# PV of the last three heads between the quarters: one decode block on one Trainium2 core

## The chip, the core and the metric

The kernel runs on one core of one Trainium2 chip. A core has a matrix engine (TensorE, PE in the profile, with its weight loads as PEld), VectorE (DVE), ScalarE (ACT), GpSimd (POOL) and SyncE (SP, which here issues nearly all DMA transfers). The engines run side by side, each works through its own queue in order, and they wait for each other through semaphores. PE reads SBUF and writes PSUM; DVE and ACT read both. The metric is device microseconds of the core. The time before is 532.45 us, the median of three runs between 530.86 and 533.08.

## The reference

One token for each of four sequences: a layer norm, then attention over the last 2048 positions of a cache of 8192 and, in parallel, a SwiGLU block, both added to the input.

```python
# B, Sq, D = 4, 1, 640;  Hq = Hkv = 32, Sk = 8192, Dh = 192;  F = 1536;  all bfloat16
W = min(4096, max(256, Sk // 4))                       # 2048
q = (x @ wq).reshape(B, Sq, Hq, Dh).transpose(0, 2, 1, 3)
k = k_cache[:, :, Sk - W:, :];  v = v_cache[:, :, Sk - W:, :]
p = _softmax(einsum("bhqd,bhkd->bhqk", q, k) * Dh ** -0.5)
o = einsum("bhqk,bhkd->bhqd", p, v)
A = o.transpose(0, 2, 1, 3).reshape(B, Sq, Hq * Dh) @ wo
Bo = (_silu(xn @ w1) * (xn @ w3)) @ w2                 # xn: layer norm of x
return x + A + Bo
```

Every head has its own keys and values: 32 heads x 4 sequences x 2048 positions x 192 numbers of two bytes, for K and for V, 201 MB of the 223 MB that the kernel reads.

## The kernel before, in words

**Layout.** A head's keys lie in one SBUF tile of 128 partitions: partition q holds 64 positions (NJ) of sequence q mod 4, 192 numbers each. Values lie alike. There are two key tiles (KBUFS) and three value tiles (VBUFS). SP issues one DMA for the keys and one for the values of a head (`load_k`, `load_v`; the values of the last and the third last head come in two halves).

**Scores.** A head is worked in four quarters of 16 positions (GQ, JQ); quarter u is head u // 4. `mult` (L231) multiplies keys by the query on DVE, `adder` (L242) adds the six 32-wide slices with six identity matmuls on PE, and `reduce_quarter` (L250) sums the last 32 on DVE. After a head's four quarters comes the softmax chain: `chain_lmax` (L254, DVE), `chain_tr` (L259, PE transpose), `chain_gmax` (L264 and L267, DVE: the maximum per sequence, and gneg, its negative scaled), `chain_bc` (L272 on PE, then L275 and the exponential L278 on ACT), and `chain_z` (L286, DVE), which spreads the weights over a one-hot of the sequence.

**PV.** `pv` (L295) multiplies the weights with the values: 24 matmuls a head, in three 32-row strips of one PSUM bank. The bank holds for each of eight positions j and four sequences all products, of which only those with the same j on both sides are wanted. `pv_diag` masks the bank (L303, o_m) and sums over j (L306, o_sb) on DVE, `ge_sum` (L322) adds the strips' sequences on PE. `ge_tot` (L311) adds the softmax denominators, `ge_rec` (L317) inverts them. Four heads form a group: `ge_turn` (L326, L328) scales and transposes (og, oT), and `ge_proj` (L212) multiplies by the group's rows of wo into the accumulator acc. `ffn_out` adds the SwiGLU block's products with w2 (L212 too) in three pieces.

**Order.** The order of work is written out by hand: `add(slot, phase, fn, ...)` puts a step into a slot, and slots are emitted one after the other, by phase within a slot. Engines keep the order of emission. There is one slot for each quarter (NU = 128) and some behind. A head's PV comes 8 slots (L) after its first quarter, mask and sum one slot later, the strip sums another slot later. The last three heads have their own places:

```python
ends = {H - 3: (NU - 3, NU - 2, NU - 1), H - 2: (NU + 2, NU + 3, NU + 4), H - 1: (NU + 6, NU + 7, NU + 7)}
```

Each triple gives the slots of PV, mask and sum, and strip sums. The last loads are issued in slot NU - 6: values of heads 30 and 31, then w2's first eight of twelve chunks, wo of the last two groups, w2's next three chunks and its last. They follow each other in one queue. At the end acc is cast to bfloat16 on DVE (L447), and two DMAs, from SP and ACT, write the two halves of the output's columns.

## Time and profile before

| | |
|---|---|
| median of three runs | 532.45 us |
| the profiled execution's own time | 533.66 us |
| its span, first to last instruction | 531.9 us |
| mean granted clock of PE | 0.89 |
| PE busy | 370.4 us, 70% |
| DVE busy | 392.5 us, 74% |
| ACT busy | 29.0 us, 5% |
| DMA, main queue, share of 16 engines | 97.7% |
| HBM read | 222.96 MB, 419 GB/s over the span |

The profile shows one execution. Busy time of an engine is an average over a start, a long even middle part of 32 heads and an end; shares say little about the end. A row such as "o_sb<-o_m 96x64 f32<-96x512 f32" names the tile written and the tile read with partitions and elements. The granted clock is the share of full speed at which PE was allowed to run. Where the text gives single times, they are us from the start of the span.

### The profile page before, as it was taken

Reading aid. Unit: us, or ns where it says so; the run is one execution under the profiler, and the core shown is the slowest. Engines: PE = TensorE matmul, PEld = TensorE weight load, DVE = VectorE, ACT = ScalarE, POOL = GpSimd, SP = SyncE. Lnnn points to the kernel's source line nnn. Section 1 sums busy time; section 2 is a strip of 40 time slices with the busy share of each in tenths; the row PEclk is TensorE's granted clock in tenths of the full one; section 3 lists DMA queues with packets and bytes.
Section 4 is the critical chain, followed back from the end, with each engine's and each line's share of the span. In section 5 each row is a group of like instructions: output and inputs, shape, how many; then the busy total and the mean of one; then the engine's idle time right before and its main releaser. Section 6 shows DMA issues by size and latency. Waiting matters only on the chain.

```text
span 531.9 us, 4826 instructions
## 1 busy us (share of the span) xinstructions
PE 370.4 (70%) x1986; PEld 143.5 (27%) x1987; DVE 392.5 (74%) x498; ACT 29.0 (5%) x110; POOL 1.1 (0%) x8
## 2 busy tenths in 40 slices
PE   2766567677658776468778676567868776876865
PEld 1322222232213322223222222223222322222323
DVE  3178776788948876887858878788768888878853
ACT  2121000000000000000000000000000000000000
POOL 0000000000000000000000000000000000000000
PEclk9989997979978889998977979899787899799777
DMA  8999999999999999999999999999999999999991
GB/s 359 440 425 432 439 427 427 433 439 421 436 429 440 425 434 426 440 425 436 429 434 429 433 430 435 426 436 433 428 433 436 429 433 434 429 434 422 431 420 48
DMA packets 11861, 223.27 MB, mean 420 GB/s; under 512 B 1328, under 2 KB 1472, under 8 KB 2624
## 3 DMA queue, kind: packets, MB, share of 16 engines
q1 hardware_dynamic: 11824, 222.97, 97.7%
q8 instruction: 15, 0.25, 0.2%
q14 instruction: 6, 0.05, 0.0%
q10 hardware_dynamic: 16, 0.01, 0.0%
HBM read 222.96 MB, written 0.01 MB: 419 GB/s over the span
## 4 chain that ended last, share of the span: by engine, by line
DMA 54%; DVE 34%; PE 10%; issue 1%; ACT 0%; SPq 0%
DMA kt<-in_A_k_cache_dram 50%; DVE pr L231 19%; DVE sc L250 5%; PE ps L242 5%; DMA wt<-in_A_wq_dram 4%; DVE o_sb L306 3%; PE o_ps L295 2%; DVE o_m L303 2%; PE qps L192 1%; DVE z L286 1%; DVE gmax L264 1%; DVE gneg L267 1%; PE acc L212 1%; DVE lmax L254 0%; DVE qbc L198 0%
## 5 line engine op out<-in xcount | busy, mean ns | idle before, releaser
L242 PE MATMUL ps<-pr,idb 128*128 128x512 bf16 x768 | 220.7, 431 | 129.0 <-DVE pr L231 128.7
L231 DVE TENSOR_TENSOR pr<-kt,qbc 128x3072 bf16<-128x3072 bf16 x128 | 223.3, 1745 | 88.4 <-DMA kt<-in_A_k_cache_dram 88.4
L242 PEld LDWEIGHTS <-idb 128*128 128x128 bf16 x768 | 78.7, 105 | 240.5 <-issue 182.3
L295 PE MATMUL o_ps<-vt,z 128*32 128x512 bf16 x768 | 100.1, 531 | 1.4 <-DMA vt<-in_A_v_cache_dram 1.4
L250 DVE TENSOR_REDUCE sc<-ps 128x16 f32<-128x512 f32 x128 | 86.8, 678 | 4.5 <-PE ps L242 4.5
L295 PEld LDWEIGHTS <-z 128*32 128x32 bf16 x768 | 32.0, 109 | 56.9 <-issue 55.1
L306 DVE TENSOR_REDUCE o_sb<-o_m 96x64 f32<-96x512 f32 x32 | 32.4, 1012 | 1.1
L275 ACT COPY negm<-mt 128x1 f32<-128x1 f32 x32 | 5.1, 159 | 449.2 <-PE mt L272 449.2
L303 DVE TENSOR_TENSOR o_m<-o_ps,jmask 96x512 f32<-96x512 f32 x32 | 21.5, 673 | 6.4 <-PE o_ps L295 6.4
L192 PE MATMUL qps<-wt,xnT 128*128 128x512 bf16 x59 | 16.1, 429 | 4.8 <-DMA wt<-in_A_wq_dram 4.8
L322 PE MATMUL po<-o_sb,sel_w 96*32 96x64 f32 x64 | 9.7, 234 | 13.2 <-DVE o_sb L306 11.2
L198 DVE CAST qbc<-qps 128x512 bf16<-128x512 f32 x6 | 3.8, 684 | 17.7 <-PE qps L192 17.7
L286 DVE TENSOR_TENSOR z<-ex,mask_b 128x256 bf16<-128x256 bf16 x32 | 13.1, 411 | 4.9 <-ACT ex L278 4.9
L272 PEld LDWEIGHTS mt<-ones_ff,gneg 1*128 1x128 f32 x64 | 9.6, 186 | 14.1 <-DVE o_m L303 10.6
L272 PE MATMUL mt<-ones_ff,gneg 1*128 1x1 f32 x64 | 12.3, 259 | 0.6 <-DVE gneg L267 0.6
L264 DVE TENSOR_REDUCE gmax<-mt 1x4 f32<-1x128 f32 x32 | 8.8, 274 | 4.8 <-PE mt L259 4.8
L278 ACT ACTIVATE ex<-sc,negm 128x64 bf16<-128x64 f32 x32 | 11.1, 348 | 1.0
L259 PE MATMUL mt<-idf,lmax 128*1 128x128 f32 x32 | 9.6, 298 | 1.1 <-DVE lmax L254 1.1
L192 PEld LDWEIGHTS <-xnT 128*128 128x128 bf16 x60 | 6.4, 107 | 14.1 <-issue 8.2
L311 PEld LDWEIGHTS po<-rsum,tot_w 128*32 128x32 f32 x64 | 5.1, 125 | 18.5 <-issue 18.1
L212 PE MATMUL acc<-wo_t,oT 128*4 128x320 bf16 x96 | 9.6, 318 | 0.0
L322 PEld LDWEIGHTS po<-o_sb,sel_w 96*32 96x32 f32 x64 | 4.4, 109 | 17.0 <-DVE o_sb L306 13.8
(54 smaller groups left out, 66.5 us busy)
## 6 DMA issues: line engine op xcount, KB each, us to landing
kt<-in_A_k_cache_dram SPq DMA_DIRECT2D x32, 3072.0 KB, 18.4
vt<-in_A_v_cache_dram SPq DMA_DIRECT2D x30, 3072.0 KB, 25.7
wo_t<-in_A_wo_dram SPq DMA_DIRECT2D x8, 960.0 KB, 19.7
wt<-in_A_wq_dram SPq DMA_DIRECT2D x2, 3072.0 KB, 13.2
vt<-in_A_v_cache_dram SPq DMA_DIRECT2D x4, 1536.0 KB, 21.1
w<-in_B_w_dram SPq DMA_DIRECT2D x2, 1920.0 KB, 30.0
wt<-in_A_wq_dram SPq DMA_DIRECT2D x1, 1536.0 KB, 19.8
w<-in_B_w_dram SPq DMA_DIRECT2D x1, 1280.0 KB, 29.4
```

The lines of the kernel that those rows point to most:

```text
L192: nc.tensor.matmul(qp[:], lhsT=xnT[:, kc].rearrange("p a b -> p (a b)"), rhs=wq_rows[kc][:, (c0 + i) * QC:(c0 + i + 1) * QC], start=(kc == ...
L212: nc.tensor.matmul(acc[i * CT:i * CT + B, :], lhsT=lhsT, rhs=rhs[:, i * N0:(i + 1) * N0], start=first, stop=last)
L231: nc.vector.tensor_tensor(out=pr[:], in0=kts[h][:, g * JQ:(g + 1) * JQ, :], in1=qbc[:, h * Dh:(h + 1) * Dh].unsqueeze(1).to_broadcast([P, ...
L242: nc.tensor.matmul(ps[:], lhsT=idb[:], rhs=pr[:, :, kk * DD:(kk + 1) * DD], start=(kk == 0), stop=(kk == NK - 1))
L250: nc.vector.tensor_reduce(out=scs[h][:, g * JQ:(g + 1) * JQ], in_=pss.pop(u)[:], axis=AX.X, op=ALU.add)
L264: nc.vector.tensor_reduce(out=gmax[:], in_=chs[h][1][0:1, 0:P].rearrange("o (p b) -> o b p", b=B), axis=AX.X, op=ALU.max)
L272: nc.tensor.matmul(mt[:, P:P + 1], lhsT=gneg[:].rearrange("o p b -> o (p b)"), rhs=ones_ff[0:1, 0:1], start=True, stop=True)
L286: nc.vector.tensor_tensor(out=z[:], in0=ex[:].unsqueeze(2).to_broadcast([P, NJ, B]), in1=mask_b[:].unsqueeze(1).to_broadcast([P, NJ, B]), ...
L295: nc.tensor.matmul(o_ps[s * CT:(s + 1) * CT].rearrange("p j c -> p (j c)"), lhsT=z[:, j:j + JG, :].rearrange("p j b -> p (j b)"), rhs=v[:, ...
L303: nc.vector.tensor_tensor(out=o_m[:], in0=o_banks[h % 2][0:SR], in1=jmask[0:SR].unsqueeze(2).to_broadcast([SR, JG, SW]), op=ALU.mult)
L306: nc.vector.tensor_reduce(out=o_sb[:], in_=o_m[:].rearrange("p j c -> p c j"), axis=AX.X, op=ALU.add)
L322: nc.tensor.matmul(po[sl, 0:SW], lhsT=sel_w[0:SR].rearrange("p a b -> p (a b)"), rhs=o_sbs.pop(h)[:], start=True, stop=True)
```

## The change

The diff has four parts. The PV of head 29 is put into four pieces of six matmuls, in slots 123 to 126, each behind the adder of the quarter before; the PV of heads 30 and 31 into two halves each, in slots 129 and 130, and 131 and 132. Mask and sum of head 29 move from slot 126 to slot 129, behind the last softmax chain's maximum; the strip sums of 29, 30 and 31 follow, the last two behind w2's first piece. (The words "row sums" in the change's name are these sums.) gneg, for all heads, moves from DVE to ACT. The masked bank is written in the order (column, j), so that the mask reads PSUM at a stride and the sum reads SBUF in order. The final cast is made in two halves, one on DVE and one on ACT.

```diff
@@ chain_gmax
-        nc.vector.tensor_scalar_mul(out=gneg[:], in0=gmax[:].unsqueeze(1).to_broadcast([1, PB, B]), scalar1=-SCALE)
+        nc.scalar.mul(out=gneg[:], in_=gmax[:].unsqueeze(1).to_broadcast([1, PB, B]), mul=-SCALE)
@@ pv_diag
-        o_m = small.tile([SR, JG, SW], FP32, tag="o_m", bufs=1, name="o_m")
-        nc.vector.tensor_tensor(out=o_m[:], in0=o_banks[h % 2][0:SR], in1=jmask[0:SR].unsqueeze(2).to_broadcast([SR, JG, SW]),
-                                op=ALU.mult)
+        o_m = small.tile([SR, SW, JG], FP32, tag="o_m", bufs=1, name="o_m")
+        nc.vector.tensor_tensor(out=o_m[:], in0=o_banks[h % 2][0:SR].rearrange("p j c -> p c j"),
+                                in1=jmask[0:SR].unsqueeze(1).to_broadcast([SR, SW, JG]), op=ALU.mult)
         o_sb = small.tile([SR, SW], FP32, tag="o_sb", bufs=2, name="o_sb")
-        nc.vector.tensor_reduce(out=o_sb[:], in_=o_m[:].rearrange("p j c -> p c j"), axis=AX.X, op=ALU.add)
+        nc.vector.tensor_reduce(out=o_sb[:], in_=o_m[:], axis=AX.X, op=ALU.add)
@@ schedule
-    ends = {H - 3: (NU - 3, NU - 2, NU - 1), H - 2: (NU + 2, NU + 3, NU + 4), H - 1: (NU + 6, NU + 7, NU + 7)}
     for h in range(H):
 ...
-        v, d, m = ends.get(h, (u0 + L, u0 + L + 1, u0 + L + 2))
-        if h < H - 1:
-            add(v, 7, pv, h)
-        else:
-            add(v - 1, 7, pv, h, 0, NJ // 2)
-            add(v, 7, pv, h, NJ // 2, NJ)
-        add(d, 8, pv_diag, h)
-        add(m, 8, ge_sum, h)
-        if h % HG == HG - 1:
-            add(m + 1, 0, ge_turn, h // HG)
-    e = ends[H - 1][2] + 1
+        if h < H - 3:
+            add(u0 + L, 7, pv, h)
+            add(u0 + L + 1, 8, pv_diag, h)
+            add(u0 + L + 2, 8, ge_sum, h)
+            if h % HG == HG - 1:
+                add(u0 + L + 3, 0, ge_turn, h // HG)
+    e = NU + 6
+    for g in range(GQ):
+        add(NU - 5 + g, 7, pv, H - 3, g * JQ, (g + 1) * JQ)
+    for g in range(2):
+        add(NU + 1 + g, 7, pv, H - 2, 2 * g * JQ, 2 * (g + 1) * JQ)
+        add(NU + 3 + g, 7, pv, H - 1, 2 * g * JQ, 2 * (g + 1) * JQ)
+    add(NU + 1, 5, pv_diag, H - 3)
+    add(NU + 2, 8, ge_sum, H - 3)
+    add(NU + 3, 8, pv_diag, H - 2)
+    add(NU + 4, 8, ffn_out, 0)
+    add(NU + 4, 8, ge_sum, H - 2)
+    add(NU + 5, 1, pv_diag, H - 1)
+    add(NU + 5, 2, ge_sum, H - 1)
+    add(e, 0, ge_turn, NG - 1)
 ...
-    add(e - 1, 7, ffn_out, 0)
-    add(e - 1, 8, ge_proj, NG - 2, 0, RPP)
+    add(e, 5, ge_proj, NG - 2, 0, RPP)
     add(e, 6, ge_proj, NG - 1, 0, RPP)
     add(e, 7, ffn_out, 1)
     add(e, 7, ffn_out, 2)
@@ end
-    nc.vector.tensor_copy(out=res[:], in_=acc[0:NR, :])
+    nc.vector.tensor_copy(out=res[:, 0:N0 // 2], in_=acc[0:NR, 0:N0 // 2])
+    nc.scalar.copy(out=res[:, N0 // 2:N0], in_=acc[0:NR, N0 // 2:N0])
```

## The prediction

> **What bounds the kernel now.** I read the page first: the DMA row stands at nine tenths or more in slices 2 to 39, and moves about 430 GB/s. Then the waits of VectorE (DVE), to see who waits for whom in the long middle part.

> ```profile
> DVE pr L231 <- DMA kt<-in_A_k_cache_dram: 88.4, 29, 7.2
> DVE o_m L303 <- PE o_ps L295: 6.4, 2, 3.9
> ```

> The columns are us in total, times, longest. DVE waits 88.4 us, in 29 heads, for keys: 3.05 us a head. Per head DMA brings 6.29 MB, 14.6 us at 430 GB/s, and the compute engines follow. What they do per head is covered by transfers, up to that reserve. The question is only what happens when the last transfers land, so third I read the issues of the last loads and their time to landing (SP's timeline puts the three w2 issues at 486.73, 494.81 and 498.5, the last wo at 487.8).

> ```profile
> L364 SPq DMA_DIRECT2D w<-in_B_w_dram x3: 328/328/584, 486.7 to 498.5; - x3
> ...
> w<-in_B_w_dram SPq DMA_DIRECT2D x1, 480.0 KB, 27.0
> w<-in_B_w_dram SPq DMA_DIRECT2D x1, 160.0 KB, 23.8
> ```

> The last number is us from issue to landing. The last piece of w2 lands at 498.5 + 23.8 = 522.3, the piece before it at 494.8 + 27.0 = 521.8, wo of the last group at 487.8 + 32.8 = 520.6. Yet the span ends at 531.9. So the last 9.6 us are not transfer: fourth, the chain of work that ended last, in order of time (start, us, what).

> ```profile
> 506.40 0.61 DVE o_m L303
> 507.03 1.01 DVE o_sb L306
> 508.63 1.68 DVE pr L231
> 515.30 1.84 PE o_ps L295 x13
> 517.35 1.55 PE o_ps L295 x9
> 518.90 0.68 DVE o_m L303
> 519.60 1.01 DVE o_sb L306
> 521.06 3.53 PE o_ps L295 x22
> 524.61 0.70 DVE o_m L303
> 525.34 1.02 DVE o_sb L306
> 526.64 2.26 PE acc L212 x31
> 528.92 0.48 DVE res L447
> ```

> The reader is to see three things. Head 29's mask and sum (506.40 to 508.04) stand ahead of the last key product (508.63). PV of head 30 does not start before 515.30, PV of head 31 not before 521.06, both back to back. And the output DMAs go out at 529.43 and end the span 2.47 us later. Fifth, the clock, in windows between its steps: us, PE busy, granted clock, DMA share, GB/s.

> ```profile
> 507.46:510.87 3.41, 0.82 (x5) 1.00 1.02 435
> 510.87:514.28 3.41, 2.10 (x6) 0.50 0.99 418
> 514.28:517.70 3.42, 2.98 (x22) 0.50 0.99 417
> 517.70:521.11 3.41, 1.50 (x14) 0.50 0.66 270
> 521.11:524.52 3.41, 3.41 (x29) 0.50 0.04 16
> ```

> After a stretch with 0.82 us of PE work the clock was 0.50 for 13.65 us, and that is where both PVs ran: 24 matmuls took 3.6 us there, against 2.93 us at 500.63, mostly at full clock.

> **The change part by part.** The page's own run took 533.66 us (span 531.9, 1.76 around it); the median of the three runs is 532.45, 1.2 below it. I work in times of the span.

> *PV 29 in four pieces.* The 24 matmuls stood between the adders of quarters 124 and 125, at 500.63. Now six go ahead of each adder of 123 to 126. The first piece is at 494.4, after head 29's row-sum matmul; its z was ready at 492.9 and its first half of V long before. At half clock six cost 0.9 us and end at 495.3; adder 123 could start at 495.2 anyway. The third needs the second half of V (landed 481.7 + 16.7 = 498.4) and comes at about 500.05, 1.6 us later. Bounds for each switch between PV and adder: nothing, or 0.15 us (one weight load at half clock, if it were not covered); the matmul rows at 500.63 and 503.49 follow without a gap, so I take nothing. Adders wait behind pieces, and DVE's sc reduces and gmax behind adders: about 0.7 us each, made up since 18 matmuls no longer stand ahead of adder 125 in one block.

> *Mask and sum of 29 behind the last quarter.* They take 0.67 + 1.01 us away from ahead of the last key product. z of head 30 (505.97) came late because its broadcast matmul stood behind all of PV 29 and adder 125 (504.89). Now: tr30 about 499.8 to 500.05, piece three to 500.8, adder 125 (1.46) to 502.25, broadcast 0.38 to 502.7, then 0.70 from its end to z as before: z at 503.4 to 503.8. Then sc 0.6, and the last product starts at 504.4 in place of 508.55.

> *From there, at full clock:* product 1.7 to 506.1; adder 1.46 to 507.6; sc 0.68, lmax 0.22, transpose 0.37 to 508.95; PV 30's first half 12 x 0.122 = 1.46 to 510.4 (its V is 3.15 MB behind 498.4, 7.3 us at 430 GB/s: an estimated 505.7); gmax and gneg run beside it; broadcast 0.38 to 510.8; PV 30's second half to 512.3, z of 31 at 511.9 beside it; two small sums, 0.5; PV 31 2.93 to 515.7 (its last V landed 486.1 + 27.0 = 513.1); w2's first 16 matmuls from their landing, 486.73 + 29.4 = 516.1, 1.44 to 517.5; mask and sum of 31 beside them; sums 0.5; og 0.28, oT 0.24: oT at 518.6. Group 6's wo product is done beside. That is 8.7 us sooner than now (527.3), and 2.0 us before the last wo lands.

> *So the loads set the end:* 12 wo matmuls from 520.6, 22 x 81 ns row: 1.0, to 521.6; six more from 521.8, 0.5; the last two from 522.3, 0.3: 522.65. Now it is 528.90: 6.25 us sooner.

> *gneg on ScalarE.* Off DVE 0.21 us a head. On ACT between 0.16 (L275, 128x1) and 0.35 (L278, 128x64); by L172 (4x1, 0.20) and L168 (4x640, 0.735) 0.83 ns an element: 0.31. Behind it wait the broadcast and, for 30, PV pieces; 0.1 longer, under an adder or a half PV. If that cover goes, 0.1 us.

> *Masked bank turned.* The sum now reads in order, the mask reads PSUM at a stride. For the stride the trace has three reduces of 128 elements:

> ```profile
> L264 DVE TENSOR_REDUCE gmax<-mt x2: 272/276/280, 106.5 to 122.1; 1x4 f32<-1x128 f32 x2
> L150 DVE TENSOR_REDUCE smask<-idf x1: 274/274/274, 2.5 to 2.5; 128x4 f32<-128x128 f32 x1
> L142 DVE TENSOR_REDUCE mask_f<-idf x1: 376/376/376, 1.8 to 1.8; 128x4 f32<-128x128 f32 x1
> ```

> Strided PSUM (L264) costs what ordered SBUF (L150) costs; strided SBUF (L142) 102 ns more. So the sum falls from 1.01 towards L250's 0.68, bounds 0.68 and 1.01, I take 0.68; the mask stays between 0.67 (same 512 elements) and 0.67 + 0.41 (102 ns x 4), I take 0.67, by the PSUM row. Worth 0.33 us on the tail, inside the 2.0 of reserve: nothing on the end.

> [...]

> *Cast in halves.* In the built order the ACT half waits on DVE alone, so it follows DVE's half, and SP's output DMA waits on ACT. DVE: 0.483 less 160 elements at 1.04 ns: 0.32; ACT: 0.16 + 160 x 0.85 ns (L200, 512 in 0.594) = 0.30; handover 0.03. Sum 0.65 against 0.48: 0.17 lost. Bounds: 0.16 won (side by side) to 0.3 lost.

> *DMA queues.* SP issues the same loads, in the same order, behind the same waits; only the output waits on ACT.

> *Sum:* 6.25 - 0.17 = about 6.0 us: span 525.9, own time 527.7, median 526.5.

> **Rivals.**
> *A, clock at half in the tail.* For: it happened at 510.87. Against: the idle 507.46 to 510.87 is filled now (adder, transpose, first half of PV 30: 2.3 us there, and windows with 2.1 to 2.8 stayed at 1.00 in this run). If it falls at 507.5 and stays: PV 30 3.6, PV 31 3.6, w2's 16 take 2.1 and each wo 1.6 (pairs of 320 columns, by L242's 512 columns in 0.43 at half clock): oT at 520.5, last matmul 524.5. 1.9 us lost: median 528.4.

> [...]

> *B, pieces stall PE.* If the second half of V 29 lands late, adders 124 to 126 and all DVE queue behind piece three. The end slips once V 29 is over 1.6 + 2.0 us late; no change within 0.5% from 7 us late (505.4). Against: it landed at 498.4, and SP's order is the same. Median 529.8 at 7 us late, and one for one beyond.

> *C, the strided mask makes DVE the bound: slower.* Place: all 32 heads. It decides once L303 exceeds the reserve: 0.67 + 3.05 + 0.21 + 0.33 = 4.3 us; each us beyond costs 29 us; the 6.0 are gone at 4.5, and at 4.8 us the median would be about 541. Nearest rows allow 1.08.

> *D, halves side by side:* the change would then do what its name says; median 526.2. Inside the forecast.

> **How the numbers follow.** A measurement tells 0.5% (2.7 us) from no change. Forecast with D 0.72, A 0.16: both faster, 0.88. B, or loads that simply end some us later, 0.08: same. Slower 0.04: C 0.02, and B with V over 12 us late 0.02. Low end: 526.5 - 0.33 (D) - 1.6 (spread of the three runs below their median) = 524.6. High end: A with 0.6 of spread, 529.0. That leaves out 2 in 10.

> **What would show it.** Right: the first PE acc matmuls on the last wo and w2 wait for DMA, not for oT; the last key product starts some 4 us sooner against the last keys' landing; L306 near 0.68, L303 near 0.67; gneg near 0.31 on ACT; ACT's cast after DVE's. Wrong: og later than the last landing; L303 over 1.1; the clock at 0.50 through both PVs; PE waiting for vt ahead of an adder.

## The result

The changed kernel took 528.22 us (median; 527.55 to 528.71), the kernel before beside it 532.77 us (530.86 to 533.16). The ratio is 0.992, 95% interval 0.9902 to 0.9937: 4.3 us less, between 3.4 and 5.2. The forecast was 526.5 us, between 524.6 and 529.0, and faster by more than 0.5%. The profiled execution took 528.39 us with a span of 526.6 us; that of before took 533.66 with 531.9.

The chain of work that ended last, in the changed kernel (start, us, what):

```profile
466.02 21.91 DMA vt<-in_A_v_cache_dram
...
487.95 33.04 DMA wo_t<-in_A_wo_dram
...
521.03 2.48 PE acc L212 x20
...
523.54 0.33 DVE res L454
...
523.89 0.28 ACT res L455
```

Both PVs, masks and sums are gone from the end of the chain. It is the load of the last group's rows of wo, the 20 matmuls that may run once it is there, and the cast. The waits from 480 us on say the same (who waited for whom: us in total, times, longest):

```profile
ACT res L455 <- DVE res L454: 13.6, 1, 13.6
...
PE acc L212 <- DMA wo_t<-in_A_wo_dram: 2.4, 2, 1.3
...
PE acc L212 <- DMA w<-in_B_w_dram: 1.5, 1, 1.5
```

In the kernel before, no matmul waited for wo or w2. The first line is the cast: ACT's half waited for DVE's. The same in order of time, lines of DVE and PE:

```profile
503.22 1.75 DVE L231 TENSOR_TENSOR pr<-kt,qbc 128x3072 bf16<-128x3072 bf16 x1
...
513.40 1.54 PE L295 MATMUL o_ps<-vt,z 128*32 128x512 bf16 x12 [0.78 <-DMA vt<-in_A_v_cache_dram]
...
516.44 0.84 PE L212 MATMUL acc<-w,hT 128*4 128x320 bf16 x10 [1.50 <-DMA w<-in_B_w_dram]
...
518.14 0.25 DVE L328 STREAM_TRANSPOSE oT<-og 128x64 bf16<-128x64 bf16 x1
518.74 0.98 PE L212 MATMUL acc<-wo_t,oT 128*4 128x320 bf16 x12 [1.05 <-DMA wo_t<-in_A_wo_dram]
...
521.03 1.40 PE L212 MATMUL acc<-wo_t,oT 128*4 128x320 bf16 x12 [1.31 <-DMA wo_t<-in_A_wo_dram]
...
522.23 1.27 PE L212 MATMUL acc<-w,hT 128*4 128x320 bf16 x8
```

The same two DVE steps in the kernel before:

```profile
508.55 1.75 DVE L231 TENSOR_TENSOR pr<-kt,qbc 128x3072 bf16<-128x3072 bf16 x1
...
527.06 0.24 DVE L328 STREAM_TRANSPOSE oT<-og 128x64 bf16<-128x64 bf16 x1
```

The last key product starts at 503.22 (before: 508.55) and oT is ready at 518.39 (before: 527.3), 2.6 us ahead of the last wo, which lands at 520.99. On its way to oT the changed kernel waits for loads too: PE waits 0.78 us for the last values, up to 513.40, and 1.50 us for w2's first piece, up to 516.44, behind which the last strip sums are placed. The last 12 wo matmuls took 1.40 us where the 12 before them took 0.98, because the clock fell under them, at 521.44. Windows (from and to in us, length; busy time and instructions of PE, PEld, DVE, ACT and POOL; granted clock, DMA share, GB/s):

```profile
519.00:521.00 2.00, 0.72 (x12) 0.35 (x7) 0.00 (x0) 0.00 (x0) 0.00 (x0) 1.00 0.53 217
521.00:523.00 2.00, 1.97 (x18) 1.06 (x19) 0.00 (x0) 0.00 (x0) 0.00 (x0) 0.61 0.16 60
```

Last, the groups that gneg and the turned bank touch, over all 32 heads, with the key product ahead of them (busy us, mean ns, then the engine's idle time ahead of them):

```profile
L231 DVE TENSOR_TENSOR pr<-kt,qbc 128x3072 bf16<-128x3072 bf16 x128 | 223.5, 1747 | 106.9 <-DMA kt<-in_A_k_cache_dram 106.9
...
L267 ACT ACTIVATE gneg<-gmax 1x128 f32<-1x128 f32 x32 | 9.8, 308 | 404.3 <-DVE gmax L264 404.3
L303 DVE TENSOR_TENSOR o_m<-o_ps,jmask 96x512 f32<-96x512 f32 x32 | 21.4, 670 | 2.7 <-PE o_ps L295 2.7
L306 DVE TENSOR_REDUCE o_sb<-o_m 96x64 f32<-96x512 f32 x32 | 21.8, 682 | 1.1
```

Mask and sum in the kernel before:

```profile
L306 DVE TENSOR_REDUCE o_sb<-o_m 96x64 f32<-96x512 f32 x32 | 32.4, 1012 | 1.1
...
L303 DVE TENSOR_TENSOR o_m<-o_ps,jmask 96x512 f32<-96x512 f32 x32 | 21.5, 673 | 6.4 <-PE o_ps L295 6.4
```

The sum takes 682 ns where it took 1012, the mask 670 where it took 673: a stride of 256 bytes in PSUM cost the mask nothing. DVE saved 32 x (0.33 + 0.21) = 17.3 us, and its idle time ahead of the key products rose from 88.4 to 106.9 us, by 18.5: what was saved in the long middle part became waiting for keys.

### The profile page after: what moved, and what is told of

It is laid out like the page before. It is cut to its first block, busy times and chain, and to the rows that moved or that the text cites. A ratio compares the mean times of both kernels' runs of the same rounds, so it can differ in the third digit from the quotient of the medians.

```text
span 526.6 us, 4829 instructions
## 1 busy us (share of the span) xinstructions
PE 357.2 (68%) x1987; PEld 140.9 (27%) x1987; DVE 374.4 (71%) x466; ACT 39.0 (7%) x143; POOL 1.1 (0%) x8
## 4 chain that ended last, share of the span: by engine, by line
DMA 63%; DVE 29%; PE 6%; ACT 1%; issue 1%; SPq 0%
DMA kt<-in_A_k_cache_dram 49%; DVE pr L231 18%; DMA wo_t<-in_A_wo_dram 6%; DVE sc L250 5%; DMA vt<-in_A_v_cache_dram 4%; DMA wt<-in_A_wq_dram 4%; PE ps L242 3%; DVE o_sb L306 2%; DVE o_m L303 2%; PE qps L192 1%; DVE z L286 1%; PE o_ps L295 1%; DVE gmax L264 1%; PE acc L212 1%; DVE lmax L254 0%
## 5 line engine op out<-in xcount | busy, mean ns | idle before, releaser
L242 PE MATMUL ps<-pr,idb 128*128 128x512 bf16 x768 | 211.1, 416 | 144.6 <-DVE pr L231 144.3
L231 DVE TENSOR_TENSOR pr<-kt,qbc 128x3072 bf16<-128x3072 bf16 x128 | 223.5, 1747 | 106.9 <-DMA kt<-in_A_k_cache_dram 106.9
L242 PEld LDWEIGHTS <-idb 128*128 128x128 bf16 x768 | 78.5, 103 | 253.6 <-issue 193.2
L295 PE MATMUL o_ps<-vt,z 128*32 128x512 bf16 x768 | 97.3, 515 | 3.2 <-DMA vt<-in_A_v_cache_dram 3.2
L250 DVE TENSOR_REDUCE sc<-ps 128x16 f32<-128x512 f32 x128 | 87.1, 680 | 2.6 <-PE ps L242 2.6
L295 PEld LDWEIGHTS <-z 128*32 128x32 bf16 x768 | 29.7, 103 | 54.5 <-issue 53.2
L267 ACT ACTIVATE gneg<-gmax 1x128 f32<-1x128 f32 x32 | 9.8, 308 | 404.3 <-DVE gmax L264 404.3
L303 DVE TENSOR_TENSOR o_m<-o_ps,jmask 96x512 f32<-96x512 f32 x32 | 21.4, 670 | 2.7 <-PE o_ps L295 2.7
L306 DVE TENSOR_REDUCE o_sb<-o_m 96x64 f32<-96x512 f32 x32 | 21.8, 682 | 1.1
L212 PE MATMUL acc<-wo_t,oT 128*4 128x320 bf16 x96 | 9.6, 319 | 2.4 <-DMA wo_t<-in_A_wo_dram 2.4
L278 ACT ACTIVATE ex<-sc,negm 128x64 bf16<-128x64 f32 x32 | 11.1, 348 | 1.0
L264 DVE TENSOR_REDUCE gmax<-mt 1x4 f32<-1x128 f32 x32 | 8.7, 273 | 2.9 <-PE mt L259 2.9
L275 ACT COPY negm<-mt 128x1 f32<-128x1 f32 x32 | 5.1, 159 | 42.6 <-PE mt L272 42.6
```

The costliest lines, as they stand in the source:

```text
L212: nc.tensor.matmul(acc[i * CT:i * CT + B, :], lhsT=lhsT, rhs=rhs[:, i * N0:(i + 1) * N0], start=first, stop=last)
L231: nc.vector.tensor_tensor(out=pr[:], in0=kts[h][:, g * JQ:(g + 1) * JQ, :], in1=qbc[:, h * Dh:(h + 1) * Dh].unsqueeze(1).to_broadcast([P, ...
L242: nc.tensor.matmul(ps[:], lhsT=idb[:], rhs=pr[:, :, kk * DD:(kk + 1) * DD], start=(kk == 0), stop=(kk == NK - 1))
L250: nc.vector.tensor_reduce(out=scs[h][:, g * JQ:(g + 1) * JQ], in_=pss.pop(u)[:], axis=AX.X, op=ALU.add)
L264: nc.vector.tensor_reduce(out=gmax[:], in_=chs[h][1][0:1, 0:P].rearrange("o (p b) -> o b p", b=B), axis=AX.X, op=ALU.max)
L278: nc.scalar.activation(out=ex[:], in_=scs.pop(h)[:], func=ACTF.Exp, bias=negm[:, 0:1], scale=SCALE, accum_out=rsum[:])
```

## The experiments

The theory was: the loads now set the end, and any compute time that is taken off behind that point is worth nothing. The rivals were that the small parts carry the gain; that the chain of work still sets the end; and that the clock, not the order, made the tail of before long. Each ratio is against the kernel before as it ran beside that kernel.

**The schedule alone (sched_only).** From the changed kernel:

```diff
-        nc.scalar.mul(out=gneg[:], in_=gmax[:].unsqueeze(1).to_broadcast([1, PB, B]), mul=-SCALE)
+        nc.vector.tensor_scalar_mul(out=gneg[:], in0=gmax[:].unsqueeze(1).to_broadcast([1, PB, B]), scalar1=-SCALE)
...
-        o_m = small.tile([SR, SW, JG], FP32, tag="o_m", bufs=1, name="o_m")
+        o_m = small.tile([SR, JG, SW], FP32, tag="o_m", bufs=1, name="o_m")
...
-    nc.vector.tensor_copy(out=res[:, 0:N0 // 2], in_=acc[0:NR, 0:N0 // 2])
-    nc.scalar.copy(out=res[:, N0 // 2:N0], in_=acc[0:NR, N0 // 2:N0])
+    nc.vector.tensor_copy(out=res[:], in_=acc[0:NR, :])
```

> The change's schedule alone; gneg on DVE, the bank's order and the whole cast as before. Theory 1 (the loads set the end of the changed kernel, and the schedule alone made room for that): the sum of head 31 is 0.33 us longer, inside the reserve of 2.6 us, and the whole cast gives 0.17 us back: median 528.0 (527.7 to 528.5), like the changed kernel or 0.2 us under it; the last wo is waited for as in the changed kernel. Rival 1 (gneg, bank order and cast carry a good part of the 4.5 us): 530 or more.

Measured: 528.44 us (527.72 to 528.61), ratio 0.9929 (0.9903 to 0.9956). Its chain:

```profile
489.76 31.07 DMA wo_t<-in_A_wo_dram
...
520.87 2.85 PE acc L212 x20
...
523.74 0.48 DVE res L454
```

The schedule brings all of the change's gain. The longer sum (1.01 us in the kernel before) lies ahead of the last landing and costs nothing.

**The three small parts alone (parts_only).** The reverse, on the kernel before:

```diff
+        nc.scalar.mul(out=gneg[:], in_=gmax[:].unsqueeze(1).to_broadcast([1, PB, B]), mul=-SCALE)
...
+        o_m = small.tile([SR, SW, JG], FP32, tag="o_m", bufs=1, name="o_m")
...
+    nc.vector.tensor_copy(out=res[:, 0:N0 // 2], in_=acc[0:NR, 0:N0 // 2])
+    nc.scalar.copy(out=res[:, N0 // 2:N0], in_=acc[0:NR, N0 // 2:N0])
```

> The schedule of before, with gneg on ACT, the turned bank and the cast in halves. Theory 1: the tail stays bound by its chain of work; three sums are 0.33 us shorter (29 ahead of the last key product, 30 ahead of PV 31, 31 ahead of the end), the halves cost 0.17, gneg 0.1 either way: 0.8 us less, median 532.0 (531.4 to 532.6). Rival 1: 530 or less.

Measured: 529.81 us (529.45 to 531.3), ratio 0.9966 (0.9953 to 0.9979): 1.8 us less, between 1.1 and 2.5, where 0.8 were expected. The time itself lies where rival 1 had put it, at 530 or less; but the schedule alone already brings the whole gain, so the small parts do not carry it. They do have a gain of their own, and it vanishes beside the schedule's: the two do not add up. Why it is 1.8 was taken up below with bank_only and gneg_only.

**Less to load, in both kernels (after_less_wo, before_less_wo).** The last group's rows of wo are not loaded, and its product takes those of the group before, so the output lacks that group's own projection:

```diff
-    add(NU - 6, 0, wo_load, NG - 1)
...
-        oT, wo_t = oTs[hg], wos[hg]
+        oT, wo_t = oTs[hg], wos[min(hg, NG - 2)]
```

> The changed kernel without the load of the last group's rows of wo, 0.98 MB (its product takes the group before's rows, so that part of the computation is changed). Theory 1 (loads set the end): 0.98 MB at 430 GB/s are 2.3 us; the last piece of w2 lands 2.3 us earlier, at about 520.4, behind oT at 518.4: 2.0 to 2.3 us less than the changed kernel, median about 526.1. Rival 2 (its own chain of work still sets the end): no change, 528.2.

Measured: 526.50 us (525.62 to 527.48), ratio 0.9897 (0.987 to 0.9924).

> The kernel before without the same load (the last group's product takes the group before's rows). Theory 1 (its chain of work sets the end, the loads are over 6 us earlier): no change, 532.8 within 0.5. Rival 3 (the loads set the end in the kernel before too, so less to load is less time): 2.3 us less, 530.5.

Measured: 532.13 us (530.25 to 533.49), ratio 1.0003 (0.9983 to 1.0024). The ends of the two chains, first the changed kernel with less to load, then the kernel before with less to load:

```profile
486.78 31.81 DMA wo_t<-in_A_wo_dram
...
518.63 3.90 PE acc L212 x32
```

```profile
524.26 1.02 DVE o_sb L306
...
525.57 2.26 PE acc L212 x31
```

0.98 MB less gave the kernel before nothing: its chain of work set the end. It gave the changed kernel 1.3 to 1.7 us (against its two medians, 527.8 and 528.2), or 1.9 against sched_only, which loads as much as the changed kernel and ran beside this one; 2.0 to 2.3 were expected. Here both groups' 24 wo matmuls wait for one load and 32 matmuls stand behind it. They took 3.90 us, from 518.63 to 522.53, and the chain shows no wait for w2's last piece among them; at the 0.98 us that 12 of them took in the changed kernel at a clock of 1.00, they would take some 2.6 (an estimate). So a part of the gain was lost to TensorE; that its clock was the reason is likely and not shown. Two of the four runs took 525.62 and 525.77, the other two 527.23 and 527.48; whether the clock is what parts them was not recorded. The sign tells the theories apart.

**The clock at the end of the changed kernel (after_again, warm).** The changed kernel once more, and with matmuls of no use in TensorE's waits for wo:

```diff
+    def warm(n):
+        for _ in range(n):
+            nc.tensor.matmul(o_banks[0][:].rearrange("p j c -> p (j c)"), lhsT=idb[:], rhs=qbc[:, 0:QC], start=True, stop=True)
...
+    add(e, 4, warm, 4)
     add(e, 5, ge_proj, NG - 2, 0, RPP)
+    add(e, 5, warm, 5)
     add(e, 6, ge_proj, NG - 1, 0, RPP)
```

> The changed kernel once more, beside the next three: 528.2 (527.7 to 528.7), to compare them with.

> The changed kernel with matmuls of no use (identity by part of the query, into a bank that is free) in TensorE's waits for the last two wo tiles, four ahead of the first and five between them, some 0.22 us each at full clock. In the changed kernel's profile the clock fell to 0.50 at 521.44 and the last 20 matmuls took 2.47 us. Theory 4 (the part of the sum that was missed at the end is the clock): it stays at 1.00, the last 20 matmuls wait for the last piece of w2 only, 0.3 to 0.6 us less: median 527.7. Rival 4 (they are bound by the landings alone): no change, 528.2, or more where the fillers stand in the way.

Measured: after_again 527.80 us (527.61 to 528.42), ratio 0.9926 (0.9905 to 0.9946); warm 527.70 us (527.66 to 528.19), ratio 0.9924 (0.9904 to 0.9944). No difference between the two can be told. The end of after_again's profile shows why:

```profile
521.04 0.98 PE L212 MATMUL acc<-wo_t,oT 128*4 128x320 bf16 x12 [1.31 <-DMA wo_t<-in_A_wo_dram]
522.24 0.71 PE L212 MATMUL acc<-w,hT 128*4 128x320 bf16 x8 [0.23 <-DMA w<-in_B_w_dram]
522.99 0.32 DVE L454 CAST res<-acc 36x160 bf16<-36x160 f32 x1 [4.59 <-PE acc L212]
```

In this execution of the same kernel the clock was at 1.00 without fillers, the 20 matmuls ended at 522.95, and the last eight waited for w2's last pieces: what the prediction's sum had laid out. In the profile shown first the 20 took 0.55 us longer. The half clock at this place came in one of this kernel's two profiles and not in the other, and the fillers can save at most that half microsecond where it comes.

**The cast in one piece (warm_cast_whole).** On top of the fillers:

```diff
-    nc.vector.tensor_copy(out=res[:, 0:N0 // 2], in_=acc[0:NR, 0:N0 // 2])
-    nc.scalar.copy(out=res[:, N0 // 2:N0], in_=acc[0:NR, N0 // 2:N0])
+    nc.vector.tensor_copy(out=res[:], in_=acc[0:NR, :])
```

> The kernel with fillers and the cast in one piece on DVE, as before. Theory: the ACT half follows the DVE half (0.33 + 0.28 + two handovers against 0.48), so one piece is 0.15 to 0.17 us faster: median 527.5, under the run with fillers alone by 0.2. Rival D (halves side by side): 0.15 slower than with fillers alone.

Measured: 527.57 us (527.41 to 527.61), ratio 0.992 (0.99 to 0.9939). Timeline lines from the cast to the output DMA, first with halves (warm), then in one piece:

```profile
522.90 0.32 DVE L460 CAST res<-acc 36x160 bf16<-36x160 f32 x1 [4.60 <-PE acc L212]
523.25 0.28 ACT L461 CAST res<-acc 36x160 bf16<-36x160 f32 x1 [12.36 <-DVE res L460]
523.56 0.30 SPq L463 DMA_DIRECT2D out_dram<-res  x1
```

```profile
522.73 0.48 DVE L460 CAST res<-acc 36x320 bf16<-36x320 f32 x1 [4.59 <-PE acc L212]
523.24 0.30 SPq L462 DMA_DIRECT2D out_dram<-res  x1
```

From cast to DMA 0.66 us in halves, 0.51 in one piece: the halves run one after the other and lose 0.15 us. The times agree: the medians are 527.70 and 527.57, and each of the five runs with one piece (527.41 to 527.61) lies below each of the five with halves (527.66 to 528.19). The ratios to the kernel before can't tell so small a difference. Of the kernels that make the whole output, this one and pv29_only (below) have the lowest medians, 0.2 us under the changed kernel's 527.80.

**The clock in the tail of before (before_warm).** Fillers alone (the same `warm`), no other edit, in the stretch from 506.8 to 510.35, where TensorE had only the small matmuls of head 29's strip sums:

```diff
+    add(NU - 1, 4, warm, 5)
+    add(NU - 1, 9, warm, 7)
```

> The kernel before with twelve such fillers in slot 127, ahead of head 30's row-sum matmul (five) and behind head 29's strip sums (seven), where TensorE waited from 506.7 to 510.35. Nothing of the schedule is changed. Theory 5 (a part of the tail of before was the half clock over PV 30 and PV 31, 13.65 us in its profile): adder 127, PV 30 and PV 31 run at full clock, 0.8 + 0.65 + 0.65 and 0.2 for the small ones: up to 2.2 us less where the clock had fallen, median 530.2 (529.5 to 531.0). Rival 5 (the order alone made the tail long): no change, 531.8 to 532.5.

Measured: 530.28 us (529.4 to 531.96), ratio 0.9973 (0.9956 to 0.9989): 1.4 us less, between 0.6 and 2.3, by work that is thrown away. Windows of PE in its profile (from and to in us, length, PE busy, granted clock, DMA share, GB/s):

```profile
510.00:512.00 2.00, 1.39 (x6) 1.00 0.97 415
512.00:514.00 2.00, 0.86 (x6) 0.95 0.99 419
514.00:516.00 2.00, 2.00 (x20) 0.50 1.01 424
516.00:518.00 2.00, 1.29 (x11) 0.69 1.01 424
518.00:520.00 2.00, 0.81 (x11) 1.00 0.75 306
```

The clock still fell, at 513.8, but for some 3.4 us and no longer for 13.65: PV 31 ran at full clock. So the clock was a part of before's long tail, and the fillers took 1.4 us of it off the median. They did not take off all of the half clock, and with them the kernel still stood 2.5 us above the changed one (530.28 against 527.80): what remains is the order and the half clock that was left, which this run does not part.

**The parts of the schedule (pv29_undone, pv29_only).** The changed kernel with head 29's part undone, and the kernel before with that part alone:

```diff
-    for g in range(GQ):
-        add(NU - 5 + g, 7, pv, H - 3, g * JQ, (g + 1) * JQ)
+    add(NU - 3, 7, pv, H - 3)
...
-    add(NU + 1, 5, pv_diag, H - 3)
-    add(NU + 2, 8, ge_sum, H - 3)
+    add(NU - 2, 8, pv_diag, H - 3)
+    add(NU - 1, 8, ge_sum, H - 3)
```

```diff
         v, d, m = ends.get(h, (u0 + L, u0 + L + 1, u0 + L + 2))
+        if h == H - 3:
+            for g in range(GQ):
+                add(NU - 5 + g, 7, pv, h, g * JQ, (g + 1) * JQ)
+            add(NU + 1, 5, pv_diag, h)
+            add(NU + 2, 8, ge_sum, h)
+            continue
```

> The changed kernel with PV 29 in one block of 24 again, between the adders of quarters 124 and 125, and head 29's mask, sum and strip sums ahead of the last key product, as before; all else as changed. Theory 1 (the reserve in front of the last loads is 2.6 us): the last key product starts 2.5 to 3.5 us later, oT at about 521.5 in place of 518.4, of which 2.6 us cost nothing: median 528.5 (528.0 to 529.5), at most 1.5 us of the 4.4 us are lost. Rival 6 (the move of PV 29 carries the gain): 530.5 or more.

Measured: 527.67 us (527.56 to 528.09), ratio 0.9914 (0.9893 to 0.9936).

```profile
506.14 1.75 DVE L231 TENSOR_TENSOR pr<-kt,qbc 128x3072 bf16<-128x3072 bf16 x1
...
520.16 0.24 DVE L328 STREAM_TRANSPOSE oT<-og 128x64 bf16<-128x64 bf16 x1
```

> The kernel before with head 29's part of the change alone: PV 29 in four pieces, its mask, sum and strip sums behind the last softmax chain's maximum. PV 30 and 31, gneg, bank and cast as before. Theory 1: the last key product starts about 4 us sooner, which takes 4 us off a tail that stands 6 us above the loads: median 529.0 (528.0 to 530.0). Rival 7 (only PV 30 and 31 in halves and the later sums help): 531.5 or more.

Measured: 527.58 us (527.47 to 527.9), ratio 0.9912 (0.9891 to 0.9933).

```profile
504.34 1.75 DVE L231 TENSOR_TENSOR pr<-kt,qbc 128x3072 bf16<-128x3072 bf16 x1
...
520.23 0.24 DVE L328 STREAM_TRANSPOSE oT<-og 128x64 bf16<-128x64 bf16 x1
```

Either gives all of the gain, since each gets oT ready by 520.4 to 520.5, some 0.4 us ahead of the last wo (matmuls on it start at 520.82 and 521.03). In pv29_only it is head 29's part alone that does it. pv29_undone still has the three small parts beside the order of heads 30 and 31; a sum that is 0.33 us longer for each of three heads could use up its 0.4 us, so that this order alone is enough is not shown. Its last key product starts 2.9 us later than in the changed kernel, as expected, and none of it was lost; I had expected up to 1.5 us. oT came only 2.0 us later, since PE no longer waited for the last values and w2's first piece. pv29_only was expected at 529.0 and came out 1.4 lower: its oT was 6.8 us ahead of before's 527.3 and not 4. The clock stayed at 1.00 through both PVs in its profile, and adder 127, PV 30 and PV 31 took 0.8, 0.7 and 0.8 us less than in before's. Both rivals fall.

**Two of the small parts (bank_only, gneg_only).** On the kernel before, one part each of parts_only's diff.

> The kernel before with the masked bank turned, alone. It is to tell why the three small parts together gave 1.8 us where 0.8 were expected. Theory 8 (three sums on the chain, 0.33 us each, and the clock as it falls): 1.0 less, median 530.9 (530.4 to 531.4). Rival 8 (the bank alone brings all of the 1.8): 530.1 or less.

Measured: 530.31 us (528.2 to 531.83), ratio 0.9951 (0.9932 to 0.9971): 2.6 us less, between 1.5 and 3.6.

> The kernel before with gneg on ACT, alone. Theory 8: 0.21 us less on DVE ahead of one quarter, 0.1 us more in the last chain: no change within 0.3, median 531.8. Rival 9 (gneg on ACT brings the missing 1 us of the three parts): 530.9 or less.

Measured: 531.91 us (530.46 to 533.77), ratio 0.9995 (0.9975 to 1.0015): no change.

The turned bank brings all of it, as rival 8 had it, and more than the three sums of 0.33 us account for (530.31 is just above the 530.1 set for rival 8, but the kernel before beside it took 532.93 and not 531.80); gneg brings nothing. Where the rest comes from is not settled. In bank_only's profile and in parts_only's the half clock fell on adder 127 and PV 30 alone and had ended before PV 31 (the clock was at 1.00 in all windows from 518 us on), where in before's it held through both (0.50 from 510.87 to 524.52); a shorter wait ahead of adder 127 might keep the clock up, as it was with the fillers (adder 127 took 1.46 us in before_warm's profile, 2.25 in before's). But gneg_only's profile has PV 31 at full clock too (1.00 from 518 us on), with no gain in its median, and one profile a kernel can't tell how often the clock falls. So that the clock brings the rest is argued, not shown.

## Why the prediction was right, and by how much it missed

*The loads set the end.* Right, shown from both sides: less to load helps the changed kernel and not the one before. The forecast of the landings (520.6 for wo, 522.3 for w2's last piece) was met within half a microsecond: 520.99 and 522.58.

*The chain up to oT.* Forecast at 518.6, measured 518.39; the last key product at 504.4, measured 503.22. The reserve was 2.6 us where I had 2.0. That oT fits so well is in part luck: the key product came 1.2 us sooner than forecast, and PE gave that back in its waits for the last values (0.78 us, where I had none) and for w2's first piece (1.50, where I had 0.4). The rearrangement was more than was needed: head 29's part would have done.

*The span and the own time.* Forecast 525.9 and 527.7. The profiled execution shown first has 526.6 and 528.39; after_again's profile 526.1 and 527.85. What is missing in the first is 0.4 us from the last wo, on which matmuls started at 521.03 and not at 520.6, and 0.4 from the clock, 0.50 from 521.44 on: the last matmuls took 2.47 us from there, where the sum had 2.05.

*The step that was off: carrying the saving over to the median.* I took 6.0 us off the profiled execution (533.66), and then the same 6.0 off a median 1.2 us below it, as if both kernels moved together. They don't. The profiled execution of before was one with the clock at half through both PVs, and its time, 533.66, lies near the top of before's runs, which lay between 529.45 and 534.04. The changed kernel, which ends with the loads, scatters less: 527.55 to 528.71. So the own time, 527.7, was the forecast for the median too. That is 1.2 of the 1.7 us that separate 526.5 from 528.22; the half clock under the last matmuls, 0.55 us in the one profile of this kernel that has it, can be the remaining 0.5.

*gneg on ACT.* 0.308 us, forecast 0.31; hidden, as forecast. *The turned bank.* Mask and sum met their forecast values (0.67, 0.68), and were worth nothing at the end beside the schedule. The stride in PSUM cost nothing here: at 64 elements the mask took 670 ns against 673.

*The cast.* One half after the other, as read from the waits: 0.15 us lost, forecast 0.17. Rival D falls.

*Rival A* came only at the very end, not in the PVs. The measured 528.22 is close to its 528.4, by chance: in the profile the clock was at 1.00 through both PVs, and oT stood 2.6 us ahead of the last wo. *Rival B* did not come, though closer than forecast: the third piece of PV 29 ran at 498.85, and its V had landed at 498.8; I had 1.6 us between them. *Rival C*: the strided mask is not slower at all.

## What to carry to other kernels

Where transfers run without a break, read from the last landings when the kernel could end, and from the chain when it does; only the difference can be won, and the first edit that closes it takes it all, so the gains of several such edits do not add up. A saving that is read from one profile belongs to that execution: if the end moves to something that varies less with the clock, forecast the new end, not the old median less the saving.

## What the runs showed that was not expected

In the changed kernel's first profile the stretch from 518.03 to 521.44 held 1.39 us of PE work, and the clock fell; in after_again's, with the same order of work, it stayed at 1.00 in every window from 514 to 524 us. The steps do not lie alike in the two profiles: counted from the start of the span, the first fall after 25 us came at 33.01 in that of before and at 33.34 in the changed kernel's. That the same wait costs time or does not, as it falls on these steps, is my reading, and no run tried it. In one set of runs the kernel before, whose tail is bound by its chain of work, scattered over 4.2 us (529.60 to 533.82), and the changed kernel, bound by loads, over 1.2 (527.55 to 528.71, in another set); that the steps of the clock are the reason is likely and not shown.

In the last stretch the loads ran at 217 GB/s and not at 430 (519 to 521 us in the changed kernel), with the 16 DMA engines busy for half of the time (0.53) on average. Why the rate falls there was not tried.
